# A gated mix of linear attention and an FFN on one core: one key-value burst tied behind the down products, a softmax and an FFN low part tied behind the fold's transposes

## The chip, the cores and the metric

The kernel runs on one core of a Trainium2 chip. The metric is the device time of one execution in microseconds (us), the median over several runs. One further execution is taken with the profiler; its rows are what this document quotes. The engines are PE (matrix multiply), DVE (vector), ACT (activation), POOL and SP (which issues the DMAs here). Each engine has a queue of its own, which it works through in the order in which the program was laid out.

## The reference

For 2048 tokens of width 512 the kernel computes a gate, an attention without a softmax over positions, and a feed-forward network (FFN):

```python
g = sigmoid((x * gate_w).sum(-1))
q, k, v = split_heads(x @ wqkv)                 # 32 heads of 16
pq, pk = q @ w_phi, k @ w_phi                   # per head
phi_q = concat(softmax(pq), softmax(-pq))       # 32 features per head
phi_k = concat(softmax(pk), softmax(-pk))
kv, z = phi_k.T @ v, phi_k.sum(positions)
a = (phi_q @ kv) / (phi_q @ z + 1e-6) @ wo
b = relu(x @ w1 + b1) ** 2 @ w2 + b2            # hidden width 1792
out = g * a + (1 - g) * b
```

All in float32.

## The kernel before, in words

Every large product is done as three matmuls (`mm3`, lines 73 to 77): each operand is split into a high part, rounded to fp32r, and a low part, the difference (`split`). ACT makes the high part and DVE the low part.

The FFN sets the frame. Tokens are cut into 4 blocks of 512, the hidden width into 14 chunks of 128; two sweeps take 7 chunks each. A step t is one chunk of one block: `do_up(t + 2)` does 12 matmuls (a tile `u` in PSUM, then on ACT a relu, a square and the high part `hh`, on DVE the low part `hl`), and `down(t, c)` for c = 0 to 3 does 12 matmuls into four banks `d`. When a block begins, those four banks must first have been emptied by the evictions of the block before (line 806).

The attention's key side runs in the first sweep. `fold` multiplies the 16 x 16 maps `w_phi` into a projection's weights: 128 small matmuls fill four banks (two of the pool of `u`, and the two of the pools `ps_a` and `ps_b` that also hold the key and value products), and four DVE transposes (line 224) bring the result to SBUF. wq's fold is put into the middle of the down products of step 9 (`FOLD_AT = 9, 3`). Keys and values of two chunks of 128 tokens (a pair p) are made by seven products in a scheme of Strassen's kind, `p1` to `p7`, in banks `kx`, `ky`, `kz`. `features` then does the dual softmax of a key chunk: four DVE passes and an exponential on ACT (`exps`), a sum and a reciprocal (`sums`), and a multiplication (`scaled`). `values` writes a value chunk into `vext` (line 564). For each pair `do_kv` adds phi_k^T v into `kvs`: 128 matmuls with 32 columns (`kv_chunk`, line 374), called here the key-value burst.

The order comes from three things. A table gives each piece of work a slot; step t traces slot 2t ahead of its up products and slot 2t + 1 behind them, and within a slot in the order of the table. A list scheduler, when the program is built, makes from this trace each engine's queue: it takes what its own cost model holds to be ready, earlier traced first, and `tc.high_priority` moves work forward by 150 instructions. And `tc.issue_after(i)` ties the instructions of a block behind instruction i where both are on the same engine; it adds no wait of its own across engines.

Before the change the kv burst of pair 0 lies in slot 17, between up 10 and down 8, tied to nothing. The softmax of key chunk 3 is done in two parts: `exps` in slot 18, right behind the product that completes the chunk, and `normed` (sum, reciprocal, multiplication) in slot 20, which is traced with its DVE work tied behind the last transpose of wq's fold. The low part of FFN step 11 is traced with its up product, ahead of the fold.

The dot product of the gate, `gate_dot` (line 320), reads a transfer of `in_xn` on DVE, and is tied behind the FFN low part traced last (`st["low"]`).

Of the kernel before, what the change touches and what calls it, by code (L numbers as in the profile page):

```python
# [8 lines left out]
F32 = mybir.dt.float32  # L9
F32R = mybir.dt.float32r  # L10
AF = mybir.ActivationFunctionType
# [26 lines left out]
def tile_gated_mix(ctx: ExitStack, tc: tile.TileContext, xT, xn, wqT, wkT, wphi, wv, wo, w1, b1, w2, b2, gw, out):  # L38
# [26 lines left out]
    def split(src, hi, lo, ehi, elo):  # L65
        if ehi is nc.scalar:
            i = nc.scalar.activation(hi, src, AF.Copy)  # L67
        else:
            i = ehi.tensor_copy(hi, src)
        st["low"] = elo.tensor_tensor(lo, src, hi.bitcast(F32), ALU.subtract)  # L70
        return i
# [269 lines left out]
    def exps(ps, tag="e"):  # L341

        pv = ps.rearrange("p (h f) -> p h f", f=DH)
        mx = small.tile([P, H], F32, tag="mx", name="mx")
        mn = small.tile([P, H], F32, tag="mn", name="mn")
        e = work.tile([P, H, 2, DH], F32, tag=tag, name="e", bufs=2 if tag == "e" else 1)
        bc = lambda t: t.unsqueeze(2).to_broadcast([P, H, DH])
        with tc.high_priority(offset=AHEAD):
            nc.vector.tensor_reduce(mx, pv, AX.X, ALU.max)
            nc.vector.tensor_reduce(mn, pv, AX.X, ALU.min)  # L350
            nc.vector.tensor_tensor(e[:, :, 0, :], pv, bc(mx), ALU.subtract)
            nc.vector.tensor_tensor(e[:, :, 1, :], bc(mn), pv, ALU.subtract)  # L352
        ef = e.rearrange("p h t f -> p (h t f)")
        nc.scalar.activation(ef, ef, AF.Exp)  # L354
        return e.rearrange("p h t f -> p (h t) f")

    def sums(e3):
        sm = small.tile([P, 2 * H], F32, tag="sm", name="sm")
        nc.vector.tensor_reduce(sm, e3, AX.X, ALU.add)  # L359
        r = small.tile([P, 2 * H], F32, tag="r", name="r")  # L360
        nc.vector.reciprocal(r, sm)
        return e3, r
# [7 lines left out]
    def kv_chunk(n, kvps, phi, v):  # L370
        for i in range(NG):
            for j in range(4):
                h = 8 * (i % 4) + 4 * (i // 4) + j
                nc.tensor.matmul(kvps[32 * j:32 * j + 32, 32 * i:32 * i + 32], v[:, h * VW:h * VW + 32],  # L374
                                 phi[:, 32 * h:32 * h + 32],
                                 start=(n % 2 == 0 and i == 0), stop=(n % 2 == 1),
                                 skip_group_check=True)
# [72 lines left out]
    def up_step(ps, k, xs, wf):  # L450
        st["up"] = mm3(ps, wf, xs[k], slice(k * P, (k + 1) * P), ALL, k == 0, k == NK - 1)

    def hidden(fc, ps):
        r = work.tile([P, SB], F32, tag="r", name="r")
        nc.scalar.activation(r, ps, AF.Relu, bias=b1c[:, fc:fc + 1])  # L455
        nc.scalar.activation(r, r, AF.Square)  # L456
        hh = work.tile([P, SB], F32R, tag="hh", name="hh", bufs=LAG + 1)
        hl = work.tile([P, SB], F32R, tag="hl", name="hl", bufs=LAG + 1)
        st["act"] = split(r, hh, hl, nc.scalar, nc.vector)
        return hh, hl  # L460

    def up(fc, xs, wf):
        ps = ps_u.tile([P, SB], F32, tag="u", name="u")
        if fc == 1 and xs is st["x", 0]:

            kk = [slice(k * P, (k + 1) * P) for k in range(NK)]
            for k in range(NK):
                for j in range(2):
                    nc.tensor.matmul(ps, wf[0][:, kk[k]], xs[k][j], start=k + j == 0, stop=False)
            for k in range(NK):  # L470
                st["up"] = nc.tensor.matmul(ps, wf[1][:, kk[k]], xs[k][0], start=False, stop=k == NK - 1)
        else:
            for k in range(NK):
                up_step(ps, k, xs, wf)
        return hidden(fc, ps)

    def down(t, c, dps):
        sw, b, i = work_list[t]
# [69 lines left out]
            mm3(ps, x, st["W", op, kk], slice(0, P), ALL, first and kk == 0, last and kk == 1, skip_group_check=True)  # L548

    def features(n, ps):  # L550
        st["e", n] = exps(ps, "ez" if n % 3 == 2 else "e")
        if n != FOLD_AT[1]:
            normed(n)

    def normed(n):
        e3, r = sums(st.pop(("e", n)))
        st["phi", n] = scaled(e3, r, nc.vector)

    def kept(tag):
# [37 lines left out]
    def p4(p):  # L597
        product(st["Y", p], p, "A22", "T4", False, True)
        t = kept("k2")
        total(t, st["Y", p], st["t1", p])  # L600
        features(2 * p + 1, t)

    def p3(p):
        product(st["Z", p], p, "S4", "B22", False, True)
# [1 line left out]

    def do_kv(p):
        ps = ps_u.tile([P, 2 * P], F32, tag="u", name="kvps")
        for m in (2 * p, 2 * p + 1):
            kv_chunk(m, ps, st["phi", m], vext[m % NV])  # L610
        with tc.high_priority(offset=AHEAD):
            nc.vector.tensor_tensor(kvs, kvs, ps, ALU.add)

# [48 lines left out]
    def at(slot, f, *a):  # L662
        steps.setdefault(int(slot), []).append(lambda: f(*a))
# [26 lines left out]
        at(made, rows_make, p)  # L690
        at(split_at, rows_ready, p)
    at(16, foldq_load)
    at(20, normed, FOLD_AT[1])
    at(20, foldq_move)
    starts = (8, 13.5, 20, 25.2, 30.4, 35.6, 40.8, 46)
    for p, s in enumerate(starts):
        todo = [(p1, s, p), (p6, s + 1, p), (p2, s + 1, p), (p5, s + 3, p)]
        if p:
            todo.append((do_kv, s + 3 + (p == 1), p - 1))
        todo += [(p7, s + 3 + (p == 1), p), (p3, s + 4, p), (p4, s + 5, p)]  # L700
        for f, slot, q in todo:
            at(slot, f, q)
    at(NB * SL - 2, do_kv, NPAIR - 1)
# [40 lines left out]
    def do_up(t):  # L744
        if t < len(work_list):
            sw, b, i = work_list[t]
            fc = sw * NFH + i
            hid[t] = up(fc, st["x", sw * NB + b], up_w[fc])

    warm_up()  # L750
    start()
# [1 line left out]
    for t, (sw, b, i) in enumerate(work_list):  # L753
        with tc.issue_after(st["turn"].ins) if t == FOLD_AT[0] + 1 else nullcontext():
            for f in steps.get(2 * t, ()):
                f()


        with tc.issue_after(st["down"].ins) if 0 < t <= LAG else nullcontext():
            fold("k") if t == 1 else do_up(t + LAG)  # L760
        for f in steps.get(2 * t + 1, ()):
            f()
        if i == 0:
            dps = [ps_d.tile([P, 512], F32, tag="d", name=f"d{c}") for c in range(NC)]


        now = () if t == last - 1 else (t - 1, t) if t == last else (t,)

        with tc.issue_after(st["up"].ins) if t < LAG else nullcontext():
            for c in range(NC):  # L770
                if t == last and c == NC - 1:
                    break
                if t == FOLD_AT[0] and c == NC // 2:
                    with tc.issue_after(st["down"].ins):
                        fold("q")
                with tc.issue_after(st["up"].ins) if t == FOLD_AT[0] and c >= NC // 2 else nullcontext():
                    for u in now:
                        down(u, c, dps)
        if t == 1:
            with tc.issue_after(st["down"].ins):  # L780
                do_up(t + LAG)
        if t == last:
            ends = [ps_u.tile([P, 512], F32, tag="u", name=f"end{j}") for j in range(2)]
            sc = slice((NC - 1) * P, NC * P)
            for j, s in enumerate(halves):
                for u in now:
                    st["down"] = mm3(ends[j][:, s], hid[u], down_w[NFH + u - last + NFH - 1], sc, s, u == now[0], u == last)
        if i < NFH - 1:
            continue
        for c in range(NC):  # L790
            n = b * NC + c
            done = ("f", n) in st
            if sw == 0:
                o = row()
                nc.scalar.activation(o, b2b, AF.Copy, scale=rest[:, n:n + 1])
            else:
                if not done:
                    st["f", n] = row()
                    nc.sync.dma_start(st["f", n], part[n])
                o = st["f", n]  # L800
            dst = part[n] if sw == 0 else out[n * P:(n + 1) * P, :]
            final = t == last and c == NC - 1
            for d, ss in [(dps[c], (ALL,))] + ([(ends[0], halves[:1]), (ends[1], halves[1:])] if final else []):
                for s in ss:
                    with tc.high_priority(offset=AHEAD):
                        nc.vector.scalar_tensor_tensor(o[:, s], d[:, s], rest[:, n:n + 1], o[:, s], ALU.mult, ALU.add)
            if final:
                for e, s in zip((nc.sync, nc.scalar), halves):
                    e.dma_start(dst[:, s], o[:, s])
            elif sw == 0 and b < NB - 1:  # L810
                at(2 * t + 3 + c // 2, lambda *a: nc.sync.dma_start(*a), dst, o)
            elif sw == 0 or done:
                nc.sync.dma_start(dst, o)
# [47 lines left out]
```

## Time and profile before

| | |
|---|---|
| median of 3 runs | 509.46 us (509.29 to 510.15) |
| profiled execution | 508.94 us |
| its span (first to last instruction) | 507.2 us |
| clock granted to PE | 0.999 of full |
| PE busy | 503.0 us (99%), 3616 matmuls |
| DVE busy | 404.0 us (80%) |
| ACT busy | 254.2 us (50%) |
| HBM traffic | 56.37 MB read, 21.50 MB written |

A row of the timeline reads: start in us from the span's start, duration in us, engine, line of the kernel, operation, output<-inputs, shapes, count, and in brackets the idle time of the engine just before with what ended it. Rows with a count merge instructions that follow each other. Matmuls overlap, so the distance between starts tells more of PE than durations.

### The profile page before, as it was taken

The numbers are of one execution on the slowest core, as the hardware profiler recorded it, in microseconds if no ns is written. First come the engines' busy times: TensorE is split into PE (matmuls) and PEld (weight loads), VectorE is DVE, ScalarE is ACT, GpSimd is POOL, SyncE is SP. The second block draws the span as 40 slices with busy tenths as digits, with TensorE's granted clock in tenths as the row PEclk, the third lists the DMA queues.
The fourth block names the chain that finished last, engine by engine and source line by source line (L and its number), as shares of the span: only waits on it lengthen the run. The fifth ranks groups of instructions, "written<-read, shape, count | busy, mean of one in ns | idle before, by whom it ended". The sixth has DMA issues, their size and how long they took to land.

```text
span 507.2 us, 9515 instructions
## 1 busy us (share of the span) xinstructions
PE 503.0 (99%) x3616; PEld 403.9 (80%) x3616; DVE 404.0 (80%) x642; ACT 254.2 (50%) x433; POOL 75.0 (15%) x77
## 2 busy tenths in 40 slices
PE   9999999999999999999999999999999999999997
PEld 4878877788888888888888878788787878788876
DVE  4979997867878777787889998978789676798724
ACT  6598571654654557273664744343525353433530
POOL 5303020202050000000004131202121212102100
PEclk9999999999999999999999999999999999999999
DMA  8899787984567656835658252213152221032102
GB/s 295 316 351 321 226 278 249 312 305 153 176 200 236 238 172 209 291 118 174 186 162 308 72 192 53 90 51 95 38 183 95 82 80 45 7 101 81 41 23 83
DMA packets 52437, 84.79 MB, mean 167 GB/s; under 512 B 8104, under 2 KB 14504, under 8 KB 52392
## 3 DMA queue, kind: packets, MB, share of 16 engines
q1 hardware_dynamic: 52072, 83.79, 51.1%
q8 instruction: 28, 0.46, 0.4%
q10 hardware_dynamic: 288, 0.39, 0.2%
q14 instruction: 17, 0.14, 0.1%
q0 software_dynamic: 32, 0.01, 0.0%
HBM read 56.37 MB, written 21.50 MB: 154 GB/s over the span
## 4 chain that ended last, share of the span: by engine, by line
PE 98%; ACT 1%; DVE 0%; issue 0%
PE d L75 10%; PE u L75 10%; PE d L77 10%; PE d L76 10%; PE u L76 10%; PE u L77 9%; PE q L75 3%; PE q L76 3%; PE q L77 3%; PE att L76 3%; PE att L77 3%; PE att L75 3%; PE ky L75 2%; PE ky L77 2%; PE ky L76 2%; PE kvps L374 2%
## 5 line engine op out<-in xcount | busy, mean ns | idle before, releaser
L455 ACT ACTIVATE r<-u,b1c 128x512 f32<-128x512 f32 x56 | 38.4, 686 | 148.8 <-PE u L77 148.8
L383 POOL TENSOR_TENSOR ez<-e,z 128x512 f32<-128x512 f32 x32 | 41.7, 1325 | 277.9 <-ACT e L354 160.5
L75 PE MATMUL d<-w2h,hh 128*128 128x512 f32 x160 | 63.1, 394 | 0.0
L77 PE MATMUL d<-w2h,hl 128*128 128x512 f32 x160 | 62.3, 390 | 0.0
L76 PE MATMUL d<-w2l,hh 128*128 128x512 f32 x160 | 62.3, 389 | 0.0
L75 PE MATMUL u<-xh,w1h 128*128 128x512 f32 x152 | 59.7, 393 | 0.1
L76 PE MATMUL u<-xl,w1h 128*128 128x512 f32 x152 | 59.2, 389 | 0.0
L77 PE MATMUL u<-xh,w1l 128*128 128x512 f32 x152 | 59.2, 389 | 0.0
L359 DVE TENSOR_REDUCE sm<-e 128x64 f32<-128x1024 f32 x32 | 38.9, 1214 | 20.3 <-ACT e L354 20.3
L70 DVE TENSOR_TENSOR hl<-r,hh 128x512 fp32r<-128x512 f32 x56 | 38.0, 678 | 16.0 <-ACT hh L67 16.0
L407 ACT ACTIVATE phiT<-tb 32x256 f32<-32x256 f32 x64 | 26.5, 413 | 32.1 <-DVE tb L401 31.5
L354 ACT ACTIVATE e<-e 128x1024 f32<-128x1024 f32 x32 | 33.8, 1055 | 12.6 <-DVE e L352 12.3
L67 ACT ACTIVATE hh<-r 128x512 fp32r<-128x512 f32 x56 | 35.3, 630 | 2.3 <-PE d L76 0.8
L456 ACT ACTIVATE r<-r 128x512 f32<-128x512 f32 x56 | 35.2, 629 | 1.3
L75 PEld LDWEIGHTS d<-w2h,hh 128*128 128x128 f32 x160 | 30.0, 188 | 6.5 <-issue 0.4
L272 POOL TENSOR_TENSOR row<-xin 128x256 f32<-128x256 f32 x16 | 17.8, 1120 | 117.4 <-DVE S4ol L70 27.6
L77 PEld LDWEIGHTS d<-w2h,hl 128*128 128x128 f32 x160 | 30.0, 188 | 6.3
L76 PEld LDWEIGHTS d<-w2l,hh 128*128 128x128 f32 x160 | 30.0, 188 | 6.0
L75 PEld LDWEIGHTS u<-xh,w1h 128*128 128x128 f32 x152 | 28.5, 188 | 7.9 <-issue 0.8
L77 PEld LDWEIGHTS u<-xh,w1l 128*128 128x128 f32 x152 | 28.5, 188 | 6.1
L76 PEld LDWEIGHTS u<-xl,w1h 128*128 128x128 f32 x152 | 28.5, 188 | 5.8
L385 DVE TENSOR_REDUCE dz<-ez 128x64 f32<-128x1024 f32 x16 | 19.4, 1210 | 9.4 <-POOL ez L383 9.3
(544 smaller groups left out, 1161.5 us busy)
## 6 DMA issues: line engine op xcount, KB each, us to landing
in<-in_w SPq DMA_DIRECT2D x66, 256.0 KB, 3.2
phiT<-tb SPq DMA_DIRECT2D x192, 32.0 KB, 1.9
w2l<-lkept SPq DMA_DIRECT2D x20, 256.0 KB, 4.0
w1l<-lkept SPq DMA_DIRECT2D x19, 256.0 KB, 3.5
xin<-in_xT SPq DMA_DIRECT2D x16, 256.0 KB, 5.7
xkept<-xh SPq DMA_DIRECT2D x16, 256.0 KB, 3.7
xkept<-xl SPq DMA_DIRECT2D x16, 256.0 KB, 4.2
in<-in_xn SPq DMA_DIRECT2D x16, 256.0 KB, 2.9
```

Source lines behind the costliest of these rows:

```text
L67: i = nc.scalar.activation(hi, src, AF.Copy)
L70: st["low"] = elo.tensor_tensor(lo, src, hi.bitcast(F32), ALU.subtract)
L75: nc.tensor.matmul(o, ah[:, sa], bh[:, sb], start=first, stop=False, **kw)
L76: nc.tensor.matmul(o, ah[:, sa], bl[:, sb], start=False, stop=False, **kw)
L77: return nc.tensor.matmul(o, al[:, sa], bh[:, sb], start=False, stop=last, **kw)
L354: nc.scalar.activation(ef, ef, AF.Exp)
L359: nc.vector.tensor_reduce(sm, e3, AX.X, ALU.add)
L383: nc.gpsimd.tensor_tensor(ez[:, hs, :], e3[:, hs, :], zbc[half], ALU.mult)
L385: nc.vector.tensor_reduce(dz, ez, AX.X, ALU.add)
L407: nc.scalar.activation(dst, src, AF.Copy)
L455: nc.scalar.activation(r, ps, AF.Relu, bias=b1c[:, fc:fc + 1])
L456: nc.scalar.activation(r, r, AF.Square)
```

## The change

Three pieces of work get another place in the queues; nothing that is computed changes.

- `do_kv` ties its 128 matmuls behind the last down product traced so far, for every pair. For pair p = 1's row of the table (whose `do_kv` works on pair 0) the slot moves from 17 to 18, and so do those of `p7` and `p3`: all of `do_kv`, `p7`, `p3`, `p4` are now in slot 18, traced ahead of up 11 and behind down 8.
- The softmax of key chunk 3 is traced as a whole at the end of slot 20, behind the transposes of wq's fold; `p4` no longer starts it.
- The low part `hl` of FFN step 11 is put aside when its up product is traced, and traced inside step 9, behind the fold's last transpose.

```diff
-    def hidden(fc, ps):
+    def hidden(fc, ps, later=False):
...
-        st["act"] = split(r, hh, hl, nc.scalar, nc.vector)
+        st["act"] = nc.scalar.activation(hh, r, AF.Copy)
+        low = lambda: st.update(low=nc.vector.tensor_tensor(hl, r, hh.bitcast(F32), ALU.subtract))
+        if later:
+            st["rest"] = low
+        else:
+            low()
         return hh, hl
...
     def features(n, ps):
-        st["e", n] = exps(ps, "ez" if n % 3 == 2 else "e")
-        if n != FOLD_AT[1]:
-            normed(n)
-
-    def normed(n):
-        e3, r = sums(st.pop(("e", n)))
+        e3, r = sums(exps(ps, "ez" if n % 3 == 2 else "e"))
         st["phi", n] = scaled(e3, r, nc.vector)
...
         total(t, st["Y", p], st["t1", p])
-        features(2 * p + 1, t)
+        if 2 * p + 1 == FOLD_AT[1]:
+            at(2 * FOLD_AT[0] + 2, features, 2 * p + 1, t)
+        else:
+            features(2 * p + 1, t)
...
     def do_kv(p):
         ps = ps_u.tile([P, 2 * P], F32, tag="u", name="kvps")
-        for m in (2 * p, 2 * p + 1):
-            kv_chunk(m, ps, st["phi", m], vext[m % NV])
+        with tc.issue_after(st["down"].ins):
+            for m in (2 * p, 2 * p + 1):
+                kv_chunk(m, ps, st["phi", m], vext[m % NV])
...
-    at(20, normed, FOLD_AT[1])
...
     for p, s in enumerate(starts):
+        late = 1.5 * (p == 1)
         todo = [(p1, s, p), (p6, s + 1, p), (p2, s + 1, p), (p5, s + 3, p)]
         if p:
-            todo.append((do_kv, s + 3 + (p == 1), p - 1))
-        todo += [(p7, s + 3 + (p == 1), p), (p3, s + 4, p), (p4, s + 5, p)]
+            todo.append((do_kv, s + 3 + late, p - 1))
+        todo += [(p7, s + 3 + late, p), (p3, s + 4 + late / 2, p), (p4, s + 5, p)]
...
-            hid[t] = up(fc, st["x", sw * NB + b], up_w[fc])
+            hid[t] = up(fc, st["x", sw * NB + b], up_w[fc], t == FOLD_AT[0] + LAG)
...
                     with tc.issue_after(st["down"].ins):
                         fold("q")
+                    with tc.issue_after(st["turn"].ins):
+                        st["rest"]()
```

More of the change, by code (lines that the diff above doesn't have):

```diff
@@ L458, in hidden, with up @@
         hl = work.tile([P, SB], F32R, tag="hl", name="hl", bufs=LAG + 1)
-        st["act"] = split(r, hh, hl, nc.scalar, nc.vector)
+        st["act"] = nc.scalar.activation(hh, r, AF.Copy)
[4 more added lines that the diff above has]
+            low()
         return hh, hl
-    def up(fc, xs, wf):
+    def up(fc, xs, wf, later):
         ps = ps_u.tile([P, SB], F32, tag="u", name="u")
@@ L474, in up @@
                 up_step(ps, k, xs, wf)
-        return hidden(fc, ps)
+        return hidden(fc, ps, later)
     def down(t, c, dps):
```

## The prediction

> **What bounds the kernel now.** I read the page's parts 1 and 4 first, then the timeline of PE over the whole span, looking at the distance from each matmul's start to the next, and then the timelines of DVE, ACT and SP around the steps that the diff touches.
>
> ```profile
> PE 503.0 (99%) x3616; PEld 403.9 (80%) x3616; DVE 404.0 (80%) x642; ACT 254.2 (50%) x433; POOL 75.0 (15%) x77
> ...
> PE 98%; ACT 1%; DVE 0%; issue 0%
> ...
> 81.47 0.39 PE L75 MATMUL d<-w2h,hh 128*128 128x512 f32 x1
> ...
> 84.19 0.39 PE L75 MATMUL ky<-T40h,xh 128*128 128x512 f32 x1
> ```
>
> PE is the bound: 99% of the span busy, and 98% of the chain that ended last is PE. But a matmul's 0.39 us overlaps its successor's, so busy time can't show what is lost. The distance of starts can: twelve down products start between 81.47 and 84.19, 0.227 us each, and that is the pace of nearly the whole span. A change makes this kernel faster only where it removes a distance longer than that, and slower only where it adds one. The diff touches two such places: the first key-value burst (73 to 79 us) and wq's fold (90 to 95 us).
>
> **The first burst.** The rows are of PE's timeline; a row's first number is its start.
>
> ```profile
> 72.89 0.39 PE L77 MATMUL u<-xh,w1l 128*128 128x512 f32 x1
> 73.20 0.26 PE L374 MATMUL kvps<-e,vext 128*32 128x32 f32 x4
> 73.39 0.50 PE L75 MATMUL d<-w2h,hh 128*128 128x512 f32 x1
> ...
> 74.28 0.26 PE L374 MATMUL kvps<-e,vext 128*32 128x32 f32 x4
> ...
> 75.36 0.25 PE L374 MATMUL kvps<-e,vext 128*32 128x32 f32 x2
> ...
> 76.43 0.25 PE L374 MATMUL kvps<-e,vext 128*32 128x32 f32 x2
> 76.61 0.50 PE L75 MATMUL d<-w2h,hh 128*128 128x512 f32 x1
> ...
> 77.50 1.20 PE L374 MATMUL kvps<-e,vext 128*32 128x32 f32 x116
> 78.63 0.50 PE L75 MATMUL ky<-T30h,S 128*128 128x512 f32 x1
> ...
> 106.91 0.39 PE L77 MATMUL kz<-T11h,S2ol 128*128 128x512 f32 x1
> 107.23 1.30 PE L374 MATMUL kvps<-e,vext 128*32 128x32 f32 x128
> 108.46 0.50 PE L75 MATMUL ky<-T30h,S2oh 128*128 128x512 f32 x1
> ...
> 251.84 0.39 PE L77 MATMUL d<-w2h,hl 128*128 128x512 f32 x1
> ...
> 253.48 0.50 PE L75 MATMUL q<-wq0h,xh 128*128 128x512 f32 x1
> ```
>
> The first burst is cut into 4, 4, 2, 2 and 116 matmuls, between the groups of three products of one down step (t = 7, which starts a new block of rows). A group should take 3 x 0.227 = 0.68 us; from the first (73.39) to the fourth (76.61) pass 3.22, 1.07 for each: four cuts of 0.39 us. The next burst (107.23) is whole, and so is the last: from the product ahead of it to the product behind it pass 108.46 - 106.91 = 1.55 and 253.48 - 251.84 = 1.64 us. In the timeline the other bursts, too, already stand behind the down step that the new line names, so for them the edit costs and brings nothing.
>
> With the edit the burst is traced in slot 18 and held behind the last product of down step 8. Expected order: down 7, down 8 (now at 81.47 to 84.19), the burst, ky T3, kz B22, ky T4, up 11. From 72.89 to the product behind the burst this takes 12 x 0.227 = 2.72 for down 7 and 1.55 to 1.64 for the whole burst, 4.27 to 4.36, where before it took 78.63 - 72.89 = 5.74 (down 8 is the same 2.72 in both, and left out). Gain 1.38 to 1.47; I take the middle, **1.43 us**. The twelve small matmuls that join the burst cost about (108.46 - 107.23) / 128 = 0.0096 us each, 0.12 in all, which is in these numbers. [...] The row of the whole burst, at under 10 ns each, is what I go by.
>
> Were the cuts filling a wait? Down 7 starts a new block, so each of its four groups needs one of the four d banks, emptied by DVE's line 806.
>
> ```profile
> 72.17 2.72 DVE L806 SCALAR_TENSOR_TENSOR row<-d,rest,row 128x512 f32<-128x512 f32 x4
> ...
> 81.26 0.68 DVE L564 TENSOR_TENSOR vext<-ky,t 128x512 f32<-128x512 f32 x1
> ...
> 85.63 0.69 DVE L320 SCALAR_TENSOR_TENSOR in<-in,gwb 128x512 f32<-128x512 f32 x1 [2.49 <-DMA in<-in_xn]
> ...
> 86.24 0.68 DVE L564 TENSOR_TENSOR k<-ky,t 128x512 f32<-128x512 f32 x1
> ```
>
> The four evictions take 2.72 in a row, 0.68 each, done at about 72.85, 73.53, 74.21 and 74.89. Uncut, the groups start at 73.12, 73.80, 74.48 and 75.16: 0.27 behind each. So the cover holds, but it is thin; every 0.1 us that the evictions come later than 0.2 costs PE 0.1. Kv issues no DMA, and SP and POOL have nothing moved past them.
>
> **The fold.** PE, then DVE, then ACT.
>
> ```profile
> 89.72 1.91 PE L209 MATMUL foldq<-row,in 32*32 32x128 f32 x128
> 91.55 0.50 PE L75 MATMUL d<-w2h,hh 128*128 128x512 f32 x1
> ...
> 92.81 0.40 PE L77 MATMUL d<-w2h,hl 128*128 128x512 f32 x1
> 93.12 0.50 PE L75 MATMUL u<-xh,w1h 128*128 128x512 f32 x1
> 93.45 0.40 PE L76 MATMUL u<-xl,w1h 128*128 128x512 f32 x1
> ...
> 93.92 0.39 PE L75 MATMUL u<-xh,w1h 128*128 128x512 f32 x1
> 94.31 0.50 PE L75 MATMUL kx<-B110h,xh 128*128 128x512 f32 x1
> 94.65 0.40 PE L76 MATMUL kx<-B110l,xh 128*128 128x512 f32 x1
> ...
> 91.75 0.69 DVE L70 TENSOR_TENSOR hl<-r,hh 128x512 fp32r<-128x512 f32 x1 [2.31 <-ACT hh L67]
> 92.36 2.50 DVE L224 STREAM_TRANSPOSE wqin<-foldq 128x512 f32<-128x512 f32 x4
> 94.78 1.17 DVE L359 TENSOR_REDUCE sm<-e 128x64 f32<-128x1024 f32 x1
> ...
> 89.47 1.06 ACT L354 ACTIVATE e<-e 128x1024 f32<-128x1024 f32 x1 [0.32 <-DVE e L352]
> ...
> 91.08 0.63 ACT L67 ACTIVATE hh<-r 128x512 fp32r<-128x512 f32 x1
> ```
>
> The fold fills four banks, and the next users of these (up 12, then kx of pair 2) wait for DVE's transposes. Those stand behind the low part hl of step 11, which waits for hh on ACT, and hh waits behind the exponential of chunk 3. So the transposes begin at 92.36, though the fold is over at 89.72 + 1.91 = 91.63. PE pays: 92.81 to 93.45 takes 0.64 for two distances, 93.92 to 94.65 takes 0.73, together 1.37 - 4 x 0.227 = **0.46 us** too much.
>
> The edit puts hl and the whole softmax of chunk 3 (its four passes over k, ahead of the fold until now, too) behind the last transpose. Then these begin when the fold ends, about 91.7, and at 0.625 each the first ends at 92.3 and the third at 93.6. PE, unhindered, asks for the first bank at 93.04 and, with four up products in between as before, for the third at 93.95. Both waits go: 0.46. Were kx queued ahead of those four products, it would ask at 93.04 for a bank free at 93.6: a wait of about 0.6 and the 0.1 of a restart, 0.25 more than now. Bounds -0.46 to +0.25; I take -0.46, since the order before the edit has the four products first and the edit only makes the bank free sooner.
>
> What moves is covered. Times in this paragraph are those of before, without the 1.43. hl of step 11 may end as early as 91.7 + 2.5 + 0.7 = 94.9, and is needed by down 11.
>
> ```profile
> 97.50 1.21 DVE L365 TENSOR_TENSOR e<-e,r 128x1024 f32<-128x1024 f32 x1
> ...
> 102.34 0.68 DVE L352 TENSOR_TENSOR e<-mn,kx 128x512 f32<-128x512 f32 x1
> 105.36 1.30 DVE L70 TENSOR_TENSOR S<-row,S 128x512 fp32r<-128x512 f32 x2 [2.34 <-ACT S L67]
> ...
> 109.95 0.40 PE L75 MATMUL d<-w2h,hh 128*128 128x512 f32 x1
> ```
>
> That is 15 us later. Behind hl come the four passes of chunk 3, 4 x 0.68 = 2.7 by the row of 102.34, its exponential, 1.06, and its sum, reciprocal and scaling, which with what lay between took 97.50 + 1.21 - 94.78 = 3.9: done at about 102.6. The burst that reads it stands at 107.23, or 106.77 when the 0.46 is gone, so there are 4.2 us of cover. DVE's idle 2.34 us before 105.36 take up most of the passes. These steps issue no DMA and pass no queue of SP or POOL. I cost them at nothing; beyond 4.2 us of lateness each us would cost PE one.
>
> **The sum.** -1.43 - 0.46 = -1.89 us. PE has no other long distance behind 110 us but changes of tile shape, so nothing waits to eat the gain. The profiled execution took 508.94 (span 507.2 and 1.74 around it), 0.52 below the median of 509.46. It becomes 507.05; the median 507.6.
>
> **Rivals.** A measurement can tell about 0.2% here, 1.02 us.
>
> Only the burst gains (0.20): another instruction takes hl's place ahead of the transposes, or kx is queued sooner. For it speaks that the order of the queues is planned afresh; against it, that both known obstacles are tied behind the last transpose. -1.43 gives 508.0; with the fold's +0.25 it would be 508.3.
>
> The burst is still cut (0.13): it is tied behind down 8, but nothing ties what comes after it, so ky T3, kz B22 or up 11 may be mixed into it. Each cut costs 0.36 net of its few matmuls; four cuts leave only the fold's 0.46, 509.0, not distinguishable from no change. Against it: all seven other bursts are whole with the same neighbours.
>
> A wait of DVE ahead of ky T4 (0.19), the slower case. With down 8 ahead, ky T3 starts at 78.63 - 1.43 + 2.72 = 79.92, and T4, 12 products later, at 82.64. T4 adds into a bank that the sum into vext (line 564) has to read first. In the rows above that sum ran at 81.26 and the gate's dot product (line 320) at 85.63, after 2.49 us of waiting for the transfer of in_xn. If the later burst lets the dot product be queued ahead of the sum, the sum waits for the transfer: the dot starts at 84.2 (if the transfer moves with PE) to 85.63, the sum 0.61 later, 0.68 long, so T4 starts at 85.5 to 86.9, 2.9 to 4.3 late. Net +1.0 to +2.4: 510.5 to 511.9. It decides from a dot product later than 83.2 on. For it: that the dot is queued ahead of a line-564 sum already (86.24). Against it: sums into vext carry the high priority of line 563, and the dot of that slot is listed behind them. [...]
>
> **How the numbers follow.** Forecast 0.48, 507.6, its own range 507.1 to 508.1 by the bounds of burst and fold. Only the burst 0.20 at 508.0; still cut 0.13 at 509.0; DVE's wait 0.19 from 510.5. Faster by over 0.2%: 0.48 + 0.20 = 0.68; within 0.2%: 0.13; slower: 0.19. The range, 506.9 to 510.5, holds the first three with some 0.2 below the forecast's own for small waits (69.74 to 73 us) that a new order may also shift, and reaches the lower end of the slower case.
>
> **What would show it.** Right: one kvps row of 128 near 78.5; down 7 in one row of 12 distances of 0.227; the transposes within 0.15 us of the fold's end, ahead of hl; no 0.50 us matmul after the six down products behind the fold; the next burst 1.9 us earlier. Wrong: a DVE row of line 320 with DMA ahead of a vext sum between 79 and 86; kvps rows under 128; a start distance over 0.3 at down 7's groups.

## The result and the profile after

The changed kernel takes 507.65 us (median of 8 executions, 506.68 to 509.44); the kernel before, beside it, 509.84 (509.29 to 510.69). The ratio is 0.9967, 95% interval 0.9954 to 0.9980: faster by 0.33%, where 507.6 was forecast. A second series gave 507.49 and 0.9963 (0.9949 to 0.9976).

The profiled execution, though, took 508.95 with a span of 507.2, the same as before. So the profile after shows what the change mended and also something that it brought. PE's timeline of the changed kernel, first at the burst, then at the fold:

```profile
72.85 0.39 PE L75 MATMUL ky<-T30h,S 128*128 128x512 f32 x1
73.08 0.39 PE L75 MATMUL d<-w2h,hh 128*128 128x512 f32 x1
...
78.61 1.30 PE L374 MATMUL kvps<-e,vext 128*32 128x32 f32 x128
79.83 0.50 PE L76 MATMUL ky<-T30l,S 128*128 128x512 f32 x1
...
82.48 0.39 PE L75 MATMUL ky<-T40h,xh 128*128 128x512 f32 x1
...
88.02 1.50 PE L209 MATMUL foldq<-row,in 32*32 32x128 f32 x96
91.86 0.51 PE L209 MATMUL foldq<-row,in 32*32 32x128 f32 x32 [2.34 <-DMA row<-in_wqT]
92.30 0.50 PE L75 MATMUL d<-w2h,hh 128*128 128x512 f32 x1
...
94.70 0.39 PE L75 MATMUL kx<-B110h,xh 128*128 128x512 f32 x1
```

The burst is one piece. 24 down products fill the time from 73.08 to 78.29 at 0.227 us each, and no group of them waits for its bank. kx of pair 2 follows the up product ahead of it (94.48) by 0.22: the wait for the transposes is gone. But the fold, which PE now reaches at 88.02 and not at 89.72, stops after 96 of its 128 matmuls for 2.34 us, until the fourth block of wqT has landed. DVE and SP of the same execution:

```profile
81.30 0.69 DVE L564 TENSOR_TENSOR vext<-ky,t 128x512 f32<-128x512 f32 x1 [0.33 <-PE ky L77]
86.13 0.69 DVE L320 SCALAR_TENSOR_TENSOR in<-in,gwb 128x512 f32<-128x512 f32 x1 [4.14 <-DMA in<-in_xn]
86.74 0.68 DVE L564 TENSOR_TENSOR vext<-kz,t 128x512 f32<-128x512 f32 x1
92.50 2.51 DVE L224 STREAM_TRANSPOSE wqin<-foldq 128x512 f32<-128x512 f32 x4 [4.47 <-PE foldq L209]
94.93 0.64 DVE L349 TENSOR_REDUCE mx<-k 128x32 f32<-128x512 f32 x1
...
76.14 1.37 SPq L200 DMA_DIRECT2D row<-in_wqT  x3
78.51 0.42 SPq L817 DMA_DIRECT2D part<-row  x1
86.37 0.33 SPq L200 DMA_DIRECT2D row<-in_wqT  x1
```

The transposes come right behind the fold, ahead of the softmax, as the change orders. SP shows where the stop is from: three blocks of wqT are loaded at 76.14, but the fourth needs the buffer that the last store of partial sums (78.51) empties; that store landed 7.8 us later, and the fourth load went out at 86.37. Before, that store went out at 80.12 and the fourth load at 86.11. The store moved 1.6 us earlier with PE; the load did not.

### The profile page after: what moved, and what is told of

Read it like the earlier page. It is cut to its first block, busy times and chain, and to the rows that moved or that the text cites. A ratio compares the mean times of both kernels' runs of the same rounds, so it can differ in the third digit from the quotient of the medians.

```text
span 507.2 us, 9518 instructions
## 1 busy us (share of the span) xinstructions
PE 500.7 (99%) x3616; PEld 404.2 (80%) x3616; DVE 404.3 (80%) x642; ACT 254.3 (50%) x433; POOL 75.5 (15%) x77
## 4 chain that ended last, share of the span: by engine, by line
PE 94%; ACT 3%; DMA 3%; issue 0%; DVE 0%; SPq 0%
PE u L75 9%; PE d L75 9%; PE d L77 9%; PE d L76 9%; PE u L76 9%; PE u L77 9%; PE q L75 3%; PE q L76 3%; PE att L77 3%; PE q L77 3%; PE att L75 3%; PE att L76 3%; PE ky L75 2%; PE ky L77 2%; PE ky L76 2%; PE kvps L374 2%
## 5 line engine op out<-in xcount | busy, mean ns | idle before, releaser
L383 POOL TENSOR_TENSOR ez<-e,z 128x512 f32<-128x512 f32 x32 | 41.8, 1328 | 278.2 <-ACT e L354 160.4
```

Source lines behind the costliest of these rows:

```text
L383: nc.gpsimd.tensor_tensor(ez[:, hs, :], e3[:, hs, :], zbc[half], ALU.mult)
```

## The experiments

As a yardstick I take from each profile the distance from the first ky of pair 1 to the start of the second burst. Start-up and the rest of the program are outside it; 144.9 to 145.5 us pass in all profiles from there to the last burst. All times are us; "before" is the median of the kernel before in the same series.

| kernel | median | before | ratio (95%) | distance in its profile |
|---|---|---|---|---|
| before | 509.84 | | | 107.23 - 63.39 = 43.8 |
| the change | 507.65 | 509.84 | 0.9967 (0.9954 to 0.9980) | 107.49 - 63.33 = 44.2 |
| e1, fold's half | 508.01 | 509.63 | 0.9971 (0.9959 to 0.9982) | 106.62 - 63.37 = 43.3 |
| e2, burst's half | 509.23 | 509.63 | 0.9998 (0.9984 to 1.0012) | 107.80 - 63.65 = 44.2 |
| e6, change + stores | 508.96 | 509.63 | 0.9990 (0.9977 to 1.0002) | 107.49 - 63.78 = 43.7 |
| e7, before + stores | 509.94 | 509.63 | 1.0008 (0.9999 to 1.0017) | 108.30 - 63.44 = 44.9 |
| the change again | 507.49 | 509.65 | 0.9963 (0.9949 to 0.9976) | 105.47 - 63.72 = 41.8 |
| e8, change + relief | 507.51 | 509.65 | 0.9959 (0.9947 to 0.9972) | 105.23 - 63.49 = 41.7 |
| e9, before, dot later | 508.82 | 509.65 | 0.9989 (0.9977 to 1.0001) | 107.08 - 63.89 = 43.2 |
| before again | 508.88 (one) | 509.65 | | 107.41 - 63.36 = 44.1 |
| e10, before + relief | 509.71 | 509.43 | 1.0010 (0.9997 to 1.0024) | 110.04 - 63.51 = 46.5 |
| e11, fold's half + relief | 508.39 | 509.43 | 0.9980 (0.9971 to 0.9989) | 107.23 - 63.91 = 43.3 |
| e12, burst's half + relief | 509.04 | 509.43 | 0.9994 (0.9982 to 1.0006) | 107.38 - 63.35 = 44.0 |
| e8 again | 507.27 | 509.43 | 0.9959 (0.9945 to 0.9973) | 105.76 - 63.83 = 41.9 |

**The halves.** e1 is the changed kernel with `do_kv` untied and its slots as before (`...` marks lines left out):

```diff
-        with tc.issue_after(st["down"].ins):
-            for m in (2 * p, 2 * p + 1):
-                kv_chunk(m, ps, st["phi", m], vext[m % NV])
+        for m in (2 * p, 2 * p + 1):
+            kv_chunk(m, ps, st["phi", m], vext[m % NV])
...
-        late = 1.5 * (p == 1)
...
+            todo.append((do_kv, s + 3 + (p == 1), p - 1))
+        todo += [(p7, s + 3 + (p == 1), p), (p3, s + 4, p), (p4, s + 5, p)]
```

> The fold's half of the change alone: low part of step 11 and softmax of chunk 3 behind the transposes; the first burst stays untied in slot 17. Theory A (the gain of the whole is 1.43 to 1.6 us from the burst plus 0.46 from the fold, and the profiled run after lost 2.34 of it to a new wait of the fold for the fourth block of wqT, whose arrival does not move with PE): PE reaches the fold no earlier than before (89.7), so the wait for wqT is 0 to 0.7, and the time is 0.2 to 0.5 us below before. Burst still cut 4, 4, 2, 2, 116. Rival B (the 2.34 us wait is a chance of the profiled run, and transfers play no part in the gain): 0.46 below before. Rival C (the fold's half brings most): over 1 us below before.

e2 is the kernel before with just those lines as in the change.

> The burst's half alone: burst tied behind down 8, slots of do_kv, p7, p3 as after; low part and softmax as before. Theory A: the burst saves 1.4 to 1.6 us, PE reaches the fold that much earlier (88.2), and there it waits for the fourth block of wqT for 0 to 2.5 us in different runs, so the time is 0 to 1.5 us below before, with a spread of runs of 2 us or more. Rival B: 1.43 below before with the spread of before (1.4 us over 8 runs). Rival C: under 0.9 below before even in the fastest runs.

The fold's half alone is 1.6 us below before, though its profile shows the cut burst; that is most of the gain. The burst's half alone gives nothing that can be measured, though its burst is whole: its median is 0.4 lower, within the spread. Rival C comes nearest, and theory A's small price of the fold is wrong; for e2 alone its 0 to 1.5 us holds too. In the profile of e2, PE and then DVE:

```profile
88.75 1.88 PE L209 MATMUL foldq<-row,in 32*32 32x128 f32 x125
91.95 0.40 PE L209 MATMUL foldq<-row,in 32*32 32x128 f32 x3 [1.32 <-issue]
...
85.59 0.69 DVE L320 SCALAR_TENSOR_TENSOR in<-in,gwb 128x512 f32<-128x512 f32 x1 [2.87 <-DMA part<-row]
92.31 0.69 DVE L70 TENSOR_TENSOR hl<-r,hh 128x512 fp32r<-128x512 f32 x1 [2.30 <-ACT hh L67]
92.92 2.50 DVE L224 STREAM_TRANSPOSE wqin<-foldq 128x512 f32<-128x512 f32 x4
```

PE is at the fold 1 us earlier and loses it there, and the transposes begin at 92.92, later than before (92.36). Their start follows the dot product of the gate (85.59) and not PE.

**The stores.** e6 is the change and e7 the kernel before, both with all four stores of a block in one slot, so that the fourth goes out ahead of wqT's loads:

```diff
-                at(2 * t + 3 + c // 2, lambda *a: nc.sync.dma_start(*a), dst, o)
+                at(2 * t + 3, lambda *a: nc.sync.dma_start(*a), dst, o)
```

> The whole change, and beside it all four stores of a block's partial sums traced in one slot (2t + 3 for every c), so that SP issues the fourth store ahead of the four loads of wqT and not behind three of them; nothing else is changed. Theory A: the fourth block of wqT lands by about 84, the fold is one piece of 128 matmuls in 1.9 us with no DMA named, the time is 1.9 to 2.7 us below before in every run, and the spread of runs shrinks to about that of before or less. Its fastest run is as the fastest of the change (506.7), its median about 0.5 to 1 us below the change's median of 507.65. Rival B: no difference from the change, 507.6, with a spread near 2.8 us.

> The kernel before with the four stores in one slot as in the experiment beside it, nothing of the change. Theory A: PE came late enough at the fold that wqT was there (its profile shows no wait), so 0 to 0.5 us below before. Rival D (the wait was already there in runs other than the profiled one): 1 us or more below before.

Both missed: e6 is 0.7 us below before, and not 1.9 to 2.7, and e7 is 0.3 above. In e6 wqT is loaded at 77.5 to 79.3 and has landed by 84.3, but the fold stops all the same, now for something else:

```profile
88.82 1.87 PE L209 MATMUL foldq<-row,in 32*32 32x128 f32 x125
91.97 0.40 PE L209 MATMUL foldq<-row,in 32*32 32x128 f32 x3 [1.29 <-issue]
...
q1 hardware_dynamic: 374, 0.68, 92.4%
q8 instruction: 1, 0.02, 3.1%
```

The last two rows are the DMA queues from 88 to 90 us. I take q8, a queue of instructions, for PE's: it has 28 packets in the whole span, 0.46 MB, for 7232 matmuls and weight loads, some 258 to a packet. The packet of this stretch began at 89.5 in e6 and at 89.4 in e2, 0.7 us behind the fold's start, and both stop when 126 of the fold's 128 weight loads are done. Two later profiles (e8 again and e12, below) have a smaller stop at the same place. There the packet began 0.6 and 0.3 us ahead of the fold, which took 2.13 and 2.38 us and not 1.9. Here are the weight loads (PEld) of e12:

```profile
88.03 1.62 PEld L209 LDWEIGHTS foldq<-row,in 32*32 32x32 f32 x126 [0.35 <-issue]
90.01 0.13 PEld L209 LDWEIGHTS foldq<-row,in 32*32 32x32 f32 x2 [0.36 <-issue]
```

In nine profiles the packet began 1.3 us or more ahead of the fold (before: 87.24 against 89.72), and none of them stops there. So I take this stop for PE waiting for its own instructions. That is an estimate by place and time, in four profiles; no experiment took that packet alone away.

The packet would also explain why e6 missed. In the first profile of the change the packet began 0.5 us ahead but took 2.7 us, until 90.2. In the four profiles the fold went on 1.2 to 1.5 us after the packet's end; by that I estimate 91.4 to 91.7, close to the 91.86 at which wqT let it go on, so removing the wait for wqT alone could bring little.

e7 points to why before varies: its dot product waits until 87.00, and PE then waits 1.27 us for the transposes (start distance 1.50 at 92.69).

**The change again, with relief, and the dot.** e8 is e6 with one more edit, the fetch of the third block of x two slots later (1 MB):

```diff
-            at((5, 17, 31)[b], x_fetch, b + 1)
+            at((5, 19, 31)[b], x_fetch, b + 1)
```

e9 is the kernel before with the dot product of chunk 5 three slots later:

```diff
-            at(s + 2, gate_dot, b * NC + c)
+            at(s + 2 + 3 * (b * NC + c == 5), gate_dot, b * NC + c)
```

> The changed kernel once more, unchanged, for a second profile and to stand beside the others on the same chip. Theory A2 (the fold's half removes a wait of 1 to 1.6 us in most executions of before; the burst's half brings PE to the fold 1.4 us earlier, and there it stops until about 91.9 for the fourth block of wqT or for PE's next block of instructions, both late while the DMA queues are full): 507 to 508.5, spread over 2 us, with a stop inside the fold that ends between 91 and 92.5. Rival E (the stop belongs to the first profile alone): no stop inside the fold.

> The whole change with two transfers given another place: the four stores of partial sums in one slot, and the fetch of the third block of x (four transfers of 256 KB) in slot 19 and not 17, which puts it on SP behind the loads of weights that precede the fold. Nothing else. Theory A2: less stands in the DMA queues at 84 to 90, wqT has landed by 84 and PE's block of instructions for the end of the fold comes within 2 us of its request; the fold is one piece or stops under 0.7 us; the distance from the first product of pair 1 (ky) to the next key-value burst falls from 44.2 in the changed kernel's profile to 42.2 to 43; 1 to 2.5 below before's median and below the change's. Rival E: same as the change.

> The kernel before with one edit: the dot product of the gate for chunk 5 three slots later, so that it no longer stands on DVE ahead of the sum that completes key chunk 3 and waits there for in_xn. Theory A2: in most executions of before that wait delays the softmax of chunk 3, its exponential, hh, hl and with them the fold's transposes by about 1 us more than in the profiled one; without it the time is 0.7 to 1.3 below before, near that of the fold's half alone (508.0). Rival F (the fold's half gains by taking hl and the exponential from in front of the transposes, and in_xn has no part in it): within 0.4 of before.

> The kernel before once more, one look, for a second profile of it. Theory A2: its up products behind the fold wait 0.5 to 1.7 us for the transposes where the first profile showed 0.46 in all, and the distance from the first ky of pair 1 to the next burst is 44 to 45. Rival F: as the first profile, 43.8.

The second profile of the change has the fold in one piece:

```profile
88.42 1.90 PE L209 MATMUL foldq<-row,in 32*32 32x128 f32 x128
90.25 0.50 PE L75 MATMUL d<-w2h,hh 128*128 128x512 f32 x1
...
92.69 0.39 PE L75 MATMUL kx<-B110h,xh 128*128 128x512 f32 x1
...
86.28 0.33 SPq L200 DMA_DIRECT2D row<-in_wqT  x1
...
row<-in_wqT SPq DMA_DIRECT2D x1, 256.0 KB, 3.3
...
90.31 2.51 DVE L224 STREAM_TRANSPOSE wqin<-foldq 128x512 f32<-128x512 f32 x4 [2.60 <-PE foldq L209]
```

The fourth block of wqT goes out at 86.28, as in the first profile (86.37), but lands after 3.3 us and not after 5.4. That is 89.6, just before the fold's last 32 matmuls ask for it. So the stop belongs to some executions and not to others (rival E as far as this one goes), and without it the distance is 41.8, 2.1 below before. With relief both profiles of the change (e8, e8 again) show 41.7 to 41.9 and no stop of the fold over 0.3; the medians of change and relief can't be told apart. e9 lies between: 0.8 below by the medians, with an interval that just holds 1. Its profile has no wait for the transposes; the share of the dot in before's loss is likely, and not settled by e9 alone. The second profile of before shows 0.47 + 0.10 + 0.17 + 0.10 = 0.84 us lost there, against 0.46.

**Do the two savings add?** The relief under before and under each half, and under the whole once more.

> The kernel before with the relief of transfers alone (four stores in one slot, fetch of the third block of x in slot 19). Theory A2 (two savings that add, of the burst 1.4 to 1.6 and of the fold 0.5 to 1.6, of which late transfers can eat): the cuts of the burst and the wait for the transposes stay, 0 to 0.8 below before; from the first ky of pair 1 to the next burst 43.3 to 44.2. Rival G (the relief itself is the gain of the earlier experiment with it): 1.5 or more below.

> The fold's half of the change with the relief of transfers, burst still cut. Theory A2: as the fold's half without relief, 507.7 to 508.5, the distance 43.2 to 43.4, since PE comes to the fold late enough for its transfers. Rival G: 1 us below that.

> The burst's half of the change with the relief of transfers; hl and the softmax of chunk 3 ahead of the transposes as before. Theory A2: without a stop inside the fold the burst's 1.4 to 1.6 shows: 0.8 to 1.6 below the kernel before with relief, 508.0 to 508.7; the distance 42.2 to 42.9, with some 0.5 of waiting for the transposes. Rival H (the burst is worth under 0.5 even so): as the burst's half without relief, 509.2.

> The whole change with the relief, once more, for its spread. Theory A2: 506.7 to 508.2 in all runs, median 507.0 to 507.6; the distance 41.7 to 41.9, the fold in one piece; if the burst and the fold add, it lies 1.9 to 2.6 below before. Rival G: as the change, with some runs over 508.5.

On top of the fold's half the burst brings 508.39 - 507.27 = 1.1 by the medians of e11 and e8 in one series, and 43.3 - 41.9 = 1.4 in the profiles. Without the relief it is 0.4 to 0.5 by the medians (e1's 508.01 against 507.65 and 507.49), within their spread. Alone it brings nothing sure (e12 0.9994, e2 0.9998; the intervals leave room for 0.9 us), where A2 expected 0.8 to 1.6 of e12.

The times don't settle that the two fail to add: the 1.6 of e1 and the 0.4 of e2 make 2.0 of the whole's 2.2. That the burst needs the fold's half is read from the rows. Those of e12 and then of e10, DVE and PE (the profiled execution of e10 is a poor one, 511.89 with a median of 509.71, and its distance of 46.5 is outside what A2 expected):

```profile
86.43 0.69 DVE L320 SCALAR_TENSOR_TENSOR in<-in,gwb 128x512 f32<-128x512 f32 x1 [3.04 <-DMA in<-in_w]
91.89 0.69 DVE L70 TENSOR_TENSOR hl<-r,hh 128x512 fp32r<-128x512 f32 x1 [1.65 <-ACT hh L67]
92.50 2.50 DVE L224 STREAM_TRANSPOSE wqin<-foldq 128x512 f32<-128x512 f32 x4
88.03 2.38 PE L209 MATMUL foldq<-row,in 32*32 32x128 f32 x128
93.26 0.50 PE L75 MATMUL u<-xh,w1h 128*128 128x512 f32 x1 [1.26 <-DVE wqin L224]
...
89.09 0.69 DVE L320 SCALAR_TENSOR_TENSOR in<-in,gwb 128x512 f32<-128x512 f32 x1 [6.05 <-ACT r L455]
95.16 2.50 DVE L224 STREAM_TRANSPOSE wqin<-foldq 128x512 f32<-128x512 f32 x4
95.93 0.50 PE L75 MATMUL u<-xh,w1h 128*128 128x512 f32 x1 [2.02 <-DVE wqin L224]
```

In e12 the fold is done at 90.4, and the transposes wait 2 us for hl. In e10 the dot runs at 89.09 and the transposes at 95.16. From the dot to the transposes pass 6.1 in both: the dot, the sum that completes k, four passes, the exponential and hh on ACT, hl. It is 6.7 before (85.63 to 92.36), where ACT's square (0.6) stands between exponential and hh, and 7.3 in e2, where the sum of kz comes in too. With hl ahead of the transposes, the time at which PE can go on is so set by when the dot runs, and PE's coming earlier doesn't move it.

That the dot waits for in_xn follows from the code, by which it reads nothing else that is new; for e2, e10 and e12 the profile names other events. e11, with the dot at 87.67, has its transposes at 91.96, right behind its fold. And the relief as such is no gain (e10: 1.0010).

## Why the prediction was right or wrong

**The first burst** (-1.43). The mechanism is as told: burst whole, down 7 uncut, no wait for the d banks. The second profile of the change, with both savings, is 2.09 shorter in the distance, against 1.89. Beyond the sum, a wait of kz at 70 us is gone, 0.15 before. But the term was counted as standing by itself, and that step failed: alone it shows no gain clear of noise (0.9998 and 0.9994), and 1.43 lies outside both intervals. PE's next bound behind the burst was not PE but two arrivals that did not come earlier with it. One is wqT. The other is the transposes by way of in_xn, which in the first profile of the change goes out at 78.03 and lands 7.9 us later, before at 79.65 and 5.8 us later. In e2, e12 and e8 again the instructions, by the estimate above, are a third.

**The fold** (-0.46). The order of the change does what was said, kx with four products ahead of it included. The size is the term that was mis-sized: worked out from one execution in which in_xn let the dot run at 85.63. For the up product behind the fold, profiles with hl ahead of the transposes show PE waiting from nothing (e9) over 0.47 (before again) and 1.27 (e7) to 2.17 (e10, the poor execution), and the fold's half measured 1.6 by the medians (e1) and 1.0 with relief (e11). Both profiled executions of before are 0.8 to 0.9 us faster than its median, and none shows a usual one; how the 1.6 is made up there stays open. So the total came out at its forecast while the parts did not: the fold gave more, the burst alone less. That 507.6 met 507.65 so closely is luck twice, in the parts and in the base: the forecast takes 1.89 from 509.46, and the kernel before measured 509.84 beside the change.

**What was missed.** For what moves, the prediction asked whose DMAs it issues. It did not ask what the fold, which moves earlier with PE, reads: wqT's fourth block, in before's profile issued at 86.11, 3.6 us ahead of the fold. "Nothing waits to eat the gain" was right behind 110 us and wrong at 90.

**The rivals.** "Only the burst gains" has it the wrong way round: alone, only the fold's half gains. The burst is not cut again. The slower case came in part: the dot is queued ahead of a sum into vext, and waits 4.14 us there, but it is the sum of kz (its last product started at 82.26, the sum at 86.74, right behind the dot), behind that of ky (81.30), and T4 started at 82.48, on time.

**The cover of 4.2 us** for chunk 3 was too generous. In the second profile of the change its last product ends at 104.30 + 1.21 = 105.51 and the burst starts at 105.47; it is saved by the burst's first half, which reads chunk 2. Passes beside POOL's rows took 1.23 to 1.25 us and not 0.68 (line 351 at 102.10), and the sum of chunk 3 started only at 99.78, behind a dot product, two low parts of x and a sum of pair 2.

```profile
93.89 1.25 DVE L351 TENSOR_TENSOR e<-k,mx 128x512 f32<-128x512 f32 x1
104.30 1.21 DVE L365 TENSOR_TENSOR e<-e,r 128x1024 f32<-128x1024 f32 x1
...
105.47 1.30 PE L374 MATMUL kvps<-e,vext 128*32 128x32 f32 x128
...
94.55 1.19 POOL L272 TENSOR_TENSOR row<-xin 128x256 f32<-128x256 f32 x1
```

**The measurement.** "Same profile, faster kernel" is no contradiction here: the two executions that were profiled first are a good one of before (508.94, its median 509.84) and a poor one of after (508.95, its median 507.65).

## What to carry to other kernels

When a bound engine is made faster ahead of a point where it meets other queues, ask for each of its next operands when it would have come if the engine had not been late; a saving is worth no more than the slack of the latest of them. Two edits that each look like a saving can hang together: by the rows here, the burst's is paid out only where the fold's cuts the chain from a transfer to the transposes. And size a wait that hangs on a transfer from more than one execution.

## What the runs showed of the hardware

In e6 and e2 PE stood inside the fold for 1.29 and 1.32 us, and the profile names nothing that it waited for (`issue`). The fold's 128 matmuls and 128 weight loads take 1.9 us and are about one packet of q8 (258 instructions, by 7232 / 28). In both profiles that packet began 0.7 us behind the fold's start, and from 88 to 90 us q1's packets took 92.4% of the DMA engines' time in e6 and (112.4 + 75.2) / 2 = 93.8% in e2. That PE had run out of instructions is my estimate from these figures; no run shows it by itself.

In the first profile of the change, three stores of 256 KB issued from 72.70 on, when the DMA engines were idle (3.5% busy from 72 to 73), landed in 2.0 us (median). The fourth, issued at 78.51, took 7.8 us, with the DMA engines 90% busy until 86.3.

In the second profile of the change, DVE's pass at 93.89 took 1.25 us and the two behind it (95.06 and 96.21) 1.23 each, where line 351 took 0.68 at 102.10, with POOL's rows done. POOL's two rows of line 272 beside them (94.55 and 95.70) took 1.19 and 1.18, the two before these (93.04 and 93.86) 0.74 each. In the first profile POOL's last row (94.98) ran beside two reductions on DVE (94.93 and 95.49), and none was longer: 0.74, 0.64 and 0.67. So some passes of the two engines took longer side by side and others did not; the rows don't show why.
